# A decayed linear-attention layer feeding a cosine-gated MLP: another written order for the steps after the first two pairs of chunks

## The chip, the cores and the metric

The kernel runs on one core of a Trainium2 chip. The metric is the device time of one launch in microseconds (us), the median of several runs. The core has five engines that run side by side, each through its own queue in order: TensorE (PE, with its weight loads shown as PEld), VectorE (DVE), ScalarE (ACT), GpSimd (POOL) and SyncE (SP), which here only issues DMAs.

## The reference

For each of 4 sequences and 8 heads a 48x48 state is decayed and added to, position by position; the outputs of all heads are put side by side and go through an MLP whose gate is `h * cos(h)`.

```python
B, H, S, D = 4, 8, 768, 48          # q, k, v, alpha: (B, H, S, D)
for t in range(S):
    state = alpha[:, :, t, :, None] * state + einsum('bhd,bhe->bhde', k[:, :, t], v[:, :, t])
    y[:, :, t] = einsum('bhd,bhde->bhe', q[:, :, t], state)
x = y.transpose(0, 2, 1, 3).reshape(B * S, H * D)   # 3072 x 384
h = x @ w_in                                        # 3072 x 2048
out = (h * cos(h)) @ w_out                          # 3072 x 384
```

## The kernel before

**Tiles.** Positions are taken 256 at a time. Such a block is one *pair* J (two chunks c = 0, 1 of 128 positions); there are 12 pairs, three to a sequence, and J runs from 0. The step names below carry the pair and, behind a dot, the chunk or part: `m2.1.0 J6` is chunk 1, part 0 of the second products of pair 6.

**The steps of a pair**, each with the engine that it runs on by default:

- `load a/k/q/v` (SP): one DMA of 384 KB for each input. `mula` (POOL) multiplies neighbouring decays, `ln` (ACT) takes their logarithm, `cums` (PE, L156 and L168) sums the logarithms, `sub` (DVE, L183) subtracts.
- `eb` (ACT): two exponentials `icp` (L193), two exponentials `exps` (L201), and the `ln` (L142) of the next pair.
- `sk.e`, `sq.e` (POOL, or DVE where the plan has `:D`; L213, L217): k and q are scaled, even and odd positions e apart. `castv` (POOL) casts v, and `vst` (SP, four DMAs) stacks it in another layout; pair 2 does the latter with `vpe` on PE and `vev`. `decay` (POOL) prepares factors.
- `trans` (PE, L259) transposes the scaled k, then the scaled q; `evT.c` copies that out of PSUM. `scores.c` (PE, L273) and `mask.c` (DVE, L278) make the masked score matrix; `outer` (PE, L290), `add.c` (DVE) and `state.c` (POOL) carry the state.
- `yT` (PE, L339) makes the attention output transposed: first the products with the state, then those with the stacked v. `evy.c` copies it to `xT`.
- `m1.u` (PE, L360, 12 matmuls, u = 0 to 3): a quarter of the first product. `sin.u` (ACT, L366) is its cosine, `gate.u` (DVE, L371) multiplies both into `gsb`.
- `m2.c.part` (PE, L389, 4 matmuls each, four parts): the product with the second weights. `evo.c` (L401) copies it out and `out.c` (SP) stores it.

**What sets the order.** It is written out by hand: `PLAN` has for each step a row with one due number for each pair, the engine letter behind a colon where it is not the default. All steps are sorted by these numbers and recorded under `manual_schedule`, so each engine's queue holds its steps in the order of the numbers. The numbers are nothing but sort keys; an engine waits at the head of its queue until the inputs and the buffer are there, and whatever stands behind waits too.

**Buffers that tie the engines.** In PSUM three two-bank buffers with the tag `h` go round among `trans`, `scores`, `outer`, `yT` and `m1`: each needs what was taken three before it to have been read out. One bank (`o`) serves `m2`, so `m2.c.0` waits for the `evo` of the chunk before. One bank (`x`) serves `cums` and `vpe`. In SBUF, `k`, `q` and `v` have three buffers each (pair J+3 loads only when pair J has been scaled or cast), `a` has four. Between loads of the tables for exponentials and for the cosine, ACT needs an `ACT_TABLE_LOAD`.

```python
    order.append((int(t), len(order), kind, args))
    ...
        for _, _, kind, args in sorted(order, key=lambda x: x[:2]):
            steps[kind](*args)
```

Of the kernel before, what the change touches and what calls it, by code (L numbers as in the profile page):

```python
# [16 lines left out]
def kernel(  # L17
# [11 lines left out]
    B, H, S, D = q.shape  # L29
# [64 lines left out]
    w1 = [consts.tile([C, KT, DF // 2], BF, tag=f"w1{r}", name="w1") for r in range(2)]  # L94
# [316 lines left out]
    def idle(n):  # L411
# [18 lines left out]


    PLAN = {
# [66 lines left out]
    }  # L499
    IDLE = [(1201, 9), (6413, 2), (7383, 14), (11727, 1), (12377, 4), (15372, 5), (16939, 5), (20459, 1)]  # L500

# [44 lines left out]
```

## Time and profile before

| | us |
|---|---|
| median of 3 runs | 183.94 |
| lowest, highest | 183.26, 184.10 |
| the profiled execution, its time | 184.12 |
| the profiled execution, its span from first to last instruction | 182.3 |
| busy: PE, DVE, ACT, POOL | 175.4, 134.8, 129.9, 71.4 |

The profiled execution's time lies 1.8 us above its span, which is what lies around the kernel's own instructions, and 0.18 us above the median. A busy engine is one with an instruction in flight; for PE the ends of matmuls are modelled, so that short waits show best as the distance between starts. The granted TensorE clock is full over the whole span.

### The profile page before, as it was taken

The numbers are of one execution on the slowest core, as the hardware profiler recorded it, in microseconds if no ns is written. First come the engines' busy times: TensorE is split into PE (matmuls) and PEld (weight loads), VectorE is DVE, ScalarE is ACT, GpSimd is POOL, SyncE is SP. The second block draws the span as 40 slices with busy tenths as digits, with TensorE's granted clock in tenths as the row PEclk, the third lists the DMA queues.
The fourth block names the chain that finished last, engine by engine and source line by source line (L and its number), as shares of the span: only waits on it lengthen the run. The fifth ranks groups of instructions, "written<-read, shape, count | busy, mean of one in ns | idle before, by whom it ended". The sixth has DMA issues, their size and how long they took to land.

```text
span 182.3 us, 5756 instructions
## 1 busy us (share of the span) xinstructions
PE 175.4 (96%) x2467; PEld 132.6 (73%) x2470; DVE 134.8 (74%) x183; ACT 129.9 (71%) x169; POOL 71.4 (39%) x104
## 2 busy tenths in 40 slices
PE   7999899989999999998999999999999999999993
PEld 2455789746697877975799669686876796787872
DVE  7188878678879897599889886978688778363460
ACT  2837687998989999959578999838964174383331
POOL 5145830377777103734894298240720320100000
PEclk9999999999999999999999999999999999999999
DMA  5999999999989959996629905690052142010032
GB/s 148 261 261 220 199 215 221 273 260 265 248 184 283 249 132 295 289 277 202 147 63 229 273 18 166 155 233 0 4 110 83 45 109 81 4 43 4 0 129 86
DMA packets 57801, 29.47 MB, mean 162 GB/s; under 512 B 50992, under 2 KB 56496, under 8 KB 57776
## 3 DMA queue, kind: packets, MB, share of 16 engines
q1 hardware_dynamic: 56256, 25.86, 58.3%
q0 software_dynamic: 1376, 3.15, 9.3%
q8 instruction: 19, 0.31, 0.7%
q10 hardware_dynamic: 144, 0.10, 0.2%
q14 instruction: 6, 0.05, 0.1%
HBM read 25.17 MB, written 4.72 MB: 164 GB/s over the span
## 4 chain that ended last, share of the span: by engine, by line
PE 77%; ACT 11%; DVE 6%; DMA 2%; issue 2%; ACTq 0%
PE h_ps L360 29%; PE o_ps L389 28%; PE y_ps L339 5%; DVE gsb L371 5%; PE idle_ps L415 4%; ACT c_sb L366 3%; PE A_ps L273 3%; PE T_ps L259 3%; DMA a<-in_alpha_dram 2%; PE U_ps L290 2%; ACT L366 2%; PE o_last L383 1%; ACT L137 1%; ACT lna L142 1%; PE cums_h L156 1%
## 5 line engine op out<-in xcount | busy, mean ns | idle before, releaser
L371 DVE TENSOR_TENSOR gsb<-h_ps,c_sb 128x1024 bf16<-128x1024 f32 x48 | 58.2, 1222 | 20.8 <-ACT c_sb L366 19.4
L366 ACT ACTIVATE c_sb<-h_ps,halfpi 128x1024 bf16<-128x1024 f32 x48 | 53.3, 1115 | 26.7 <-PE h_ps L360 26.4
L389 PE MATMUL o_ps<-w,gsb 128*128 128x384 bf16 x368 | 67.1, 327 | 0.6 <-DVE o_sb L401 0.6
L360 PE MATMUL h_ps<-xT,w 128*128 128x256 bf16 x576 | 67.0, 273 | 0.3 <-issue 0.2
L360 PEld LDWEIGHTS <-w 128*128 128x128 bf16 x576 | 62.4, 114 | 2.5 <-DMA w<-in_moe_w_in_dram 0.3
L389 PEld LDWEIGHTS <-gsb 128*128 128x128 bf16 x368 | 33.9, 98 | 21.4 <-issue 1.1
L312 POOL TENSOR_TENSOR un<-us,c 128x384 bf16<-128x384 f32 x20 | 16.8, 838 | 46.2 <-DVE us L304 36.9
L278 DVE TENSOR_TENSOR A_sb<-A_ps,msk 128x1024 bf16<-128x1024 f32 x24 | 28.9, 1216 | 3.4 <-PE A_ps L273 3.4
L217 POOL TENSOR_TENSOR qh<-q,cp 128x384 bf16<-128x384 f32 x13 | 13.8, 1063 | 13.3 <-ACT cp L201 12.2
L213 POOL TENSOR_TENSOR kh<-k,icp 128x384 bf16<-128x384 f32 x15 | 14.9, 1007 | 2.4 <-ACT icp L193 1.0
L220 POOL CAST vp<-v 128x768 bf16<-128x768 f32 x12 | 9.9, 827 | 12.0 <-DMA v<-in_v_dram 12.0
L150 POOL TENSOR_TENSOR a<-a 128x384 f32<-128x384 f32 x9 | 9.0, 1003 | 10.1 <-DMA a<-in_alpha_dram 10.1
L142 ACT ACTIVATE lna<-a 128x768 bf16<-128x768 f32 x12 | 10.1, 844 | 3.5 <-DMA a<-in_alpha_dram 3.3
L415 PE MATMUL idle_ps<-zeros 128*128 128x512 bf16 x38 | 11.1, 439 | 1.4 <-DVE halfpi L77 1.2
L401 ACT COPY o_sb<-o_ps 128x384 f32<-128x384 f32 x13 | 6.2, 478 | 8.5 <-PE o_ps L389 8.5
L137 ACT ACT_TABLE_LOAD x9 | 11.5, 1283 | 0.9 <-PEq L530 0.7
L366 ACT ACT_TABLE_LOAD x9 | 11.5, 1283 | 0.2
L304 DVE TENSOR_TENSOR us<-U_ps,un 128x384 f32<-128x384 f32 x16 | 8.8, 551 | 3.8 <-POOL un L312 2.1
L265 ACT COPY qkT<-T_ps 128x1024 bf16<-128x1024 bf16 x10 | 9.8, 1016 | 1.9 <-PE T_ps L259 1.8
L217 DVE TENSOR_TENSOR qh<-q,cp 128x384 bf16<-128x384 f32 x11 | 6.8, 629 | 5.4 <-DMA q<-in_q_dram 5.3
L265 DVE COPY qkT<-T_ps 128x1024 bf16<-128x1024 bf16 x14 | 9.4, 680 | 1.2 <-PE T_ps L259 1.2
L273 PE MATMUL A_ps<-qkT 48*128 48x128 bf16 x192 | 9.0, 217 | 0.7 <-DVE gsb L371 0.5
(70 smaller groups left out, 156.6 us busy)
## 6 DMA issues: line engine op xcount, KB each, us to landing
a<-in_alpha_dram SPq DMA_DIRECT2D x12, 384.0 KB, 5.9
q<-in_q_dram SPq DMA_DIRECT2D x12, 384.0 KB, 6.1
k<-in_k_dram SPq DMA_DIRECT2D x12, 384.0 KB, 6.0
v<-in_v_dram SPq DMA_DIRECT2D x12, 384.0 KB, 6.3
out_dram<-o_sb SPq DMA_DIRECT2D x23, 192.0 KB, 3.5
vs<-vp SPq DMA_DIRECT2D x36, 64.0 KB, 2.8
w<-in_moe_w_in_dram POOLq DMA_DIRECT2D x2, 768.0 KB, 9.6
w<-in_moe_w_out_dram POOLq DMA_DIRECT2D x4, 384.0 KB, 8.7
```

The costliest lines, as they stand in the source:

```text
L137: nc.scalar.preload_act_table_set("natural_log_exp_and_others")
L213: eng.tensor_tensor(out=kh_t[J % NQ][:, e, :, 0:D], in0=kqv["k", J][:, :, e], in1=icp_, op=ALU.mult)
L217: eng.tensor_tensor(out=qh_t[J % NQ][:, e, :, 0:D], in0=kqv["q", J][:, :, e], in1=cp, op=ALU.mult)
L265: copy(out=qkT_sb[J][:, c], in_=T_ps[J][:, c].rearrange("r n e s -> r n (e s)"))
L273: nc.tensor.matmul(A_ps[J, c][:, a, p, :], qkT[r, c, NP + p, :], qkT[r, c, p, :], start=True, stop=True)
L278: nc.vector.tensor_tensor(out=A_sb[J][:, c].rearrange("s a p t -> s (a p) t"), in0=A_ps.pop((J, c)).rearrange("s a p t -> s (a p) t"), in1 ...
L312: nc.gpsimd.tensor_tensor(out=u, in0=U_sum.pop(n), in1=c2_sb[J][:, :, c].unsqueeze(3).to_broadcast([C, NP, 2, D]), op=ALU.mult)
L360: nc.tensor.matmul(h_ps[J, u][:, f, :], cols, xT[J][:, kk, :], start=(kk == 0), stop=(kk == KT - 1))
L366: nc.scalar.activation(out=c_sb[J, u], in_=h_ps[J, u], func=AF.Sin, bias=halfpi, scale=1.0)
L371: nc.vector.tensor_tensor(out=gsb[J][:, u * FW : (u + 1) * FW], in0=h_ps.pop((J, u)), in1=c_sb.pop((J, u)), op=ALU.mult)
L389: nc.tensor.matmul(o_ps[J, c][:, 0:DM], gsb[J][:, ft, c * C : (c + 1) * C], w2[:, ft], start=(ft == 0), stop=(ft == NF - 1))
L415: nc.tensor.matmul(idle_ps[0], zeros[:, 0:C], zeros, start=True, stop=True)
```

## The change

Only numbers and engine letters in `PLAN` differ: no step is added or taken away, no instruction has another shape. (The number of `w1` for pair 3 stands for nothing: `load_w1` returns for u above 1.) What it does:

- **Queue of PE, pairs 0 to 3.** `m1.2`, `m1.0`, `m1.1` of pair 1 come before the first `m2` of pair 0. `trans J2` goes ahead of `m2.0.0 J1`, `m2.0.1 J1` and `m2.0.2 J1`; `scores.1 J2`, `vpe`, `outer J2`, `trans J3` follow later. `cums J5` goes behind `m1.0 J2`.
- **Queue of PE, later.** `scores.1 J4` goes ahead of `m2.0.3 J2`; `cums J8` and `cums J11` go one `m2` block back; `outer J10` goes ahead of `scores.1 J11`; `m2.0.0 J10` goes ahead of `yT J11`. All else keeps its order.
- **DVE and ACT** exchange some copies: `evy.1` of pairs 1, 2, 8, `evy.0` of pairs 4, 10, `evT.0` of pairs 2, 10, `evo.0` of pairs 2, 8 and `evo.1 J9` go to DVE, `evo.1` of pairs 4, 8, `evo.0` of pairs 7, 9 and `evy.1 J9` to ACT. `gate.3 J1` now stands ahead of `evo.1 J0` on DVE.
- **POOL and DVE** exchange some scalings: `sk.0 J2`, `sq.0 J6`, `sk.1 J5`, `sq.0 J5`, `sq.1 J5`, `sq.0 J10`, `sk.1 J10`, `sq.1 J11` go to POOL, `sk.1 J3`, `sq.0 J3`, `sq.0 J9`, `sq.0 J11`, `sk.1 J11` to DVE (`sq.1 J3` to POOL).
- **SP**: loads, stacking copies and stores come in another order from the eleventh DMA on.

```diff
-        "load a": "750 2205 4425 24496 25066 37693 43693 45193 55293 56793 62293 70470",
-        "load k": "3345 7425 31693 34693 40693 52193 64033 73545 85258 93648 94218 114101",
-        "load q": "2775 8925 25636 36193 42193 52763 54533 63463 72180 78488 96723 113531",
-        "load v": "5925 10425 33193 39193 46693 64693 71040 71610 94788 95358 117164 132675",
+        "load a": "750 1320 4425 24496 31693 37693 42193 47393 55293 56793 60346 72793",
+        "load k": "2925 7425 25636 36193 45893 52893 65893 67033 84648 94083 97988 113396",
+        "load q": "1890 8925 25066 34693 40693 44393 54633 60916 71293 78478 93513 99488",
+        "load v": "5925 10425 33193 39193 54063 66463 70043 74293 85218 94653 95823 119529",
...
-        "cums": "5885 11199 13924 36668 44122 49975 61282 73275 86251 91443 105424 117024",
+        "cums": "5885 11199 13924 36015 44673 52476 61147 73140 86769 91308 105289 117542",
...
-        "sk 0": "9160:D 14846:D 39112:D 41953:D 48949 58577 77428:D 89268 92888 110613 111733 130015",
-        "sk 1": "9909:D 13739:D 38528 41528 47999 59591:D 73470 88318 91938 107448 124627:D 130965",
-        "sq 0": "7660:D 15296:D 37028:D 43028 52978 60646:D 77878:D 84607 93838 103437 116334:D 127345",
+        "sk 0": "9160:D 14846:D 37028 43028:D 55578 58442 77681:D 89133 92923 111493 112443 125569",
+        "sk 1": "9909:D 13739:D 37978 43478:D 52728 62842 74222 88183 91973 109423 121602 129221:D",
+        "sq 0": "7660:D 15296:D 35528:D 41528:D 54628 60162 77398 84472 93873 103302:D 114343 127138:D",
...
-        "castv": "12160 17628 40028 46545 56778 71528 75880 90218 100558 104387 129245 144989",
+        "castv": "12160 17628 40028 46500 59392 72502 76628 90083 96553 100423 123332 143936",
...
-        "trans": "10624 16461 40648 44533 57020 68793 81884 90868 108663 115899 126133 137709",
+        "trans": "10624 16461 39163 44098 56885 68658 81749 90733 108528 115764 125998 137574",
...
-        "evy 0": "19246 24739 49715 59116:D 72412 90700:D 90225:D 109076:D 125077:D 140194:D 150737 162583",
-        "evy 1": "18876 25109 49345 58036:D 72782 89595:D 90795 110156:D 124397 139114:D 150367 162953",
+        "evy 0": "19246 24739 49217 58506:D 72777:D 90565:D 90090:D 108941:D 124967:D 139939:D 151513:D 162978",
+        "evy 1": "18876 26020:D 48647:D 58981:D 72277 89460:D 90660 110021:D 124492:D 139204 150232 163348",
...
-        "gate 3": "27509 39826 56896 64334 79468 101000 112696 113876 137657 146554 162724 174200",
-        "m2 0 0": "28796 39247 55547 69368 82679 99651 110556 124292 136308 150139 162355 172851",
+        "gate 3": "27509 38291 56761 64114 79752 100865 112561 113741 137522 146419 162589 174065",
+        "m2 0 0": "31432 40041 55412 69233 82544 99516 110421 124157 136173 150004 161240 172716",
...
-        "evo 0": "34574:D 44322 62603 73475 85575 103280:D 116004 128413:D 140515 153925:D 165167:D 176969",
-        "evo 1": "38637:D 54119 68348:D 81659 92173:D 108601:D 123512 133462 144087:D 157621 171423 178295:D",
+        "evo 0": "34244:D 43548 61201:D 73728 85440 103752:D 115869 128079 140414:D 153556 165032:D 176834",
+        "evo 1": "39431:D 53684 68213:D 81524 91030 108466:D 123377 133327 143952 157486:D 168962 178160:D",
```

In the stretch that the change orders most freely, PE's queue reads as follows (before, then after):

```
m2.1.3 J0 | m2.0.0 m2.0.1 J1 | trans outer vpe.1 J2 | m2.0.2 J1 | vpe.0 scores.1 J2 | m2.0.3 J1 | cums J4 trans J3 scores.0 J2 | m2.1.0 m2.1.1 J1 | scores.0 J3 | m2.1.2 J1 | yT J2 scores.1 outer J3 | m2.1.3 J1 | cums J5 | m1 J2 ...
m2.1.3 J0 | trans J2 | m2.0.0 m2.0.1 m2.0.2 J1 | scores.1 vpe.1 J2 | m2.0.3 J1 | vpe.0 outer J2 trans J3 cums J4 | m2.1.0 J1 | scores.0 J2 scores.0 J3 | m2.1.1 m2.1.2 J1 | yT J2 scores.1 outer J3 | m2.1.3 J1 | m1.1 m1.0 J2 | cums J5 | m1 J2 ...
```

86 rows, old and new, of the table PLAN are left out of this document.

## The prediction

> **What bounds the kernel now.** I read the page's busy line and clock first, then the waits of PE, then the timeline of PE around each wait, and only then the other engines and the landings of the loads.
>
> ```profile
> PE 175.4 (96%) x2467; PEld 132.6 (73%) x2470; DVE 134.8 (74%) x183; ACT 129.9 (71%) x169; POOL 71.4 (39%) x104
> ...
> PEclk9999999999999999999999999999999999999999
> ```
>
> PE is the bound and runs at the full clock, so an order can gain only what PE spends waiting. The waits of PE behind the start (the head of the kernel, up to 21 us, keeps its order) are few:
>
> ```profile
> PE o_ps L389 <- DVE o_sb L401: 0.6, 1, 0.6
> PE A_ps L273 <- DVE gsb L371: 0.5, 1, 0.5
> ...
> PE U_ps L290 <- ACT xT L350: 0.3, 1, 0.3
> PE A_ps L273 <- DVE qkT L265: 0.2, 1, 0.2
> ```
>
> The two long ones in the timeline of PE (start, us, idle before it in brackets):
>
> ```profile
> 37.27 1.46 PE L389 MATMUL o_ps<-w,gsb 128*128 128x384 bf16 x8
> 39.38 1.46 PE L389 MATMUL o_ps<-w,gsb 128*128 128x384 bf16 x8 [0.65 <-DVE o_sb L401]
> ...
> 82.19 0.41 PE L259 MATMUL T_ps<-ident_bf,qh 64*128 64x64 bf16 x16
> 83.09 0.40 PE L273 MATMUL A_ps<-qkT 48*128 48x128 bf16 x8 [0.49 <-DVE gsb L371]
> ```
>
> By starts: eight products of `m2` take 1.40 us (39.38 to 40.78, where `trans J2` begins), so `m2.0.0 J1` could have begun at 37.27 + 1.40 = 38.67; it began at 39.38. The wait is 0.71. It is for the one `o` bank: `evo.1 J0` ran from 38.77 to 39.33. Scores follow a transpose's second half by 0.23 elsewhere (116.81 to 117.04), so `scores.1 J5` could have begun at 82.42; it began at 83.09, 0.67 late. Beyond these there are about 0.25 us at 117.4 and 0.16 at 25.1. All the waiting that an order could save behind the head is about 1.8 us, 1% of the time, while a new wait has no such cap.
>
> **Part 1, the front (38.7 to 50 us): a loss of 0.39.** The 48 first products and 32 second ones up to 38.67 change places, but I find each one's buffer in time: `m1.2 J1` at 27.9 needs `evy.1 J1`, now behind `gate.0 J0` (end 26.60) plus 0.59; `m1.0 J1` at 29.2 needs `gate.3 J0` (29.13); `m1.1 J1` at 30.5 needs `gate.2 J0` (30.44); `m2.0.2 J0` at 33.15 needs weights that landed at 33.03. Each margin is 0.05 to 0.7, and what slips here is caught by the wait that follows. Then `trans J2` comes ahead of `m2.0.0 J1`. Its k and q no longer wait behind two decay loads: q J2 and k J2 land in the second and third place, 35.65 and 37.10 (the slots in which alpha 4 and q J2 landed). POOL then does `sk.0 J2` and `sk.1 J2` from 37.13 at 1.00 us each, so PE may begin `trans J2` at 39.15 and spends 0.56 on it (68.88 to 69.44 in the trace). The `o` bank comes later than before, because `gate.3 J1` now stands ahead of `evo.1 J0` on DVE. ACT sets its time:
>
> ```profile
> 36.13 1.28 ACT L366 ACT_TABLE_LOAD   x1
> 37.42 1.11 ACT L366 ACTIVATE c_sb<-h_ps,halfpi 128x1024 bf16<-128x1024 f32 x1
> ```
>
> The cosine ends at 38.53, the gate takes 1.22 and ends at 39.8, `evo.1 J0` takes 0.56 with 0.08 of overlap and ends at 40.28, `m2.0.0 J1` begins at 40.33. PE's wait is 40.33 − 38.67 − 0.56 = 1.10 instead of 0.71: +0.39. Queued behind `evo.1 J0` are `evT.0 J2` and `evT.1 J2` (0.69 each, done at 41.7), which `scores.1 J2` wants at 42.4; `sk.0 J3` and `sk.1 J3` on DVE, with k J3 landing at 42.93, are done at 44.0 and `trans J3` wants them at 44.4; `yT J2` wants `mask.0 J2` at 47.9 and gets it at 47.4. The later pieces are the same work with as many changes of shape, so I see neither a second loss nor a gain up to `m1 J2`. Bounds: 0 (if the gate were to slip in earlier) to +0.7 (if k J3 is half a load slot late).
>
> **Part 2, the DVE queue at 77 us: a gain of 0.67.** What releases `scores.1 J5` is `gate.2 J4`, last of a row on DVE:
>
> ```profile
> 77.67 0.88 DVE L213 TENSOR_TENSOR kh<-k,icp 128x384 bf16<-128x384 f32 x1
> 78.47 1.18 DVE L217 TENSOR_TENSOR qh<-q,cp 128x384 bf16<-128x384 f32 x1
> 79.56 3.47 DVE L371 TENSOR_TENSOR gsb<-h_ps,c_sb 128x1024 bf16<-128x1024 f32 x3
> ...
> 78.39 0.84 POOL L220 CAST vp<-v 128x768 bf16<-128x768 f32 x1 [0.26 <-DMA v<-in_v_dram]
> ```
>
> The 1.18 us are `sq.0 J6`, which takes 0.56 when POOL is idle; it goes to POOL. Without it the gates of u = 0 and 3 follow at 78.5 and 79.7; the one of u = 2 waits for its cosine (79.75 + 1.11 = 80.86) and ends at 82.1, 0.3 before PE wants it at 82.42. So the wait goes entirely. Next late is nothing on DVE: `mask.1 J5` ends 0.6 ahead of `scores.0 J6`. The Trainium skill says in SBUF — State Buffer, "Who interferes with whom", that a DVE instruction with two SBUF inputs and a GpSimd instruction that reads SBUF lock each other out for a whole instruction. The trace agrees: `sq.0 J6` began 0.08 us behind a POOL cast of 0.84 and took 1.18, about the cast's rest and itself without its start-up. By the rule `sk.0 J6`, which stays, would fall to 0.56 too, which makes the gain safer and no larger.
>
> **Part 3, exchanged copies and queues moved past: a loss of 0.1, another 0.1 for the loads.** `evy.0 J4` on DVE waits for `evy.1 J4` on ACT, as both write one tile (at 91.3 us the trace shows the like: ACT waits 0.3 us for a DVE copy of `xT`). So 0.58 on ACT and 0.59 on DVE follow each other from 72.54 and `m1.1 J4` gets its input at 73.75, where PE came at 73.65: +0.1. The other exchanged copies have room: `evo.0 J8` 0.2 us, `evo.0 J7` 0.8, `evy.0 J10` over 2. The moved `cums` cost nothing (0.27 us between two `m2` blocks at 106.13 as in the row of others at 118.00), nor does `m2.0.0 J10` ahead of `yT J11`, whose copies are wanted 1.5 us later.
>
> On POOL, `sq.0 J6` now stands behind `castv J6`, which waits for v J6, and on SP the load of q J9 waits for `sq.0 J6`, and behind it stand one store and the eight stacking DMAs `vst J6` and `vst J5`. Before, v J6 landed at 78.33, the eight began at 81.84, and the last landed at 89.29; `yT J5` used it at 89.76. Afterwards v J6 has as many loads ahead (24) but two more stores, 0.57 us each (59.39 to 59.96). Against that, q J7 and alpha 10 go ahead of `vst J4`, so the hole of about 1.5 us that SP left in the transfers near 66 us (alpha 10 issued at 64.48, landed at 69.39) gets smaller. I take 78.8, between 78.3 and 79.4. Then `castv J6` and `sq.0 J6` end at 80.6, q J9 and the store are issued by 81.9, and the last stacked v lands at about 89.3, while PE, 0.3 us ahead of before, wants it at 89.5. Cost 0.1, bounds 0 and 0.4. Where k J4 comes three slots later (47.83 to about 52.6), POOL's four scalings end at 56.65 and `trans J4` wants them at 57.3.
>
> **The sum:** +0.39 − 0.67 + 0.1 + 0.1 = −0.08 on the profiled 184.12, so 184.04, and 183.9 at the median, which lies 0.18 lower. Two real changes cancel. About 0.5% (0.9 us) is what a measurement of this kernel can tell from no change.
>
> **Rivals.** First, slower: the chain v J6, `castv J6`, `sq.0 J6`, q J9, `vst J6`, `vst J5`, `yT J5`. It decides once v J6 lands after 79.1; from there every us goes to PE. One load slot (1.45 us) behind my 78.8 gives 80.25, so about 1.1 more; one and a half with `trans J6` itself late gives 185.2 to 185.6. For it: landings in the trace slip by 1 to 1.6 us now and then (q J6 came 2.6 us behind the store ahead of it). Against it: the shorter hole. 185.2, chance 0.20.
>
> Second, a wait that changes place: `sq.0 J9` is now on DVE ahead of `evo.0 J5`. It may begin at 104.3 (`exps` 103.76 + 0.52), end at 104.85, `evo.0 J5` at 105.35, and `m2.1.0 J5` comes at 105.47. It decides if a POOL cast of v J9 runs just then: 0.65 more, 184.5. v J9 is now the third load behind `vst J7`, a slot that landed at 103.12, and the cast ends at 104.0. By the lock rule named above this would be the full 0.65. Chance 0.08.
>
> Third, faster: the front costs nothing, since PE begins `trans J2` in its wait and the pieces behind it join better, and the transfers do no harm: 183.9 − 0.39 − 0.2 = 183.3, less if the wait at 117.4 goes as well (183.0). Against it: the ACT row is fixed by the landing of alpha 3, which stays. Chance 0.08.
>
> **How the numbers follow.** My forecast has 0.64, with 183.3 to 184.5 of its own from the bounds of its terms. Faster by over 0.5% means below 183.0: most of the third rival, 0.06. Slower by over 0.5% means above 184.9: the first rival and 0.04 of the forecast's own tail, 0.24. The rest, 0.70, lies within. The range 183.1 to 185.3 leaves out about a tenth on either side.
>
> **What would show it.** `m2.0.0 J1` at 40.3 behind an `evo` that follows `gate.3 J1`, with two waits of PE that make 1.1 us; no wait of `scores.1 J5` at 82; `m1.1 J4` waiting under 0.15; v J6 landed before 79.1. A wait of PE over 0.3 us anywhere from 42 to 82 us, or at `yT J5`, would make me wrong.

## The result, and the profile after

The changed kernel takes **184.17 us** (median of 20 runs, 183.62 to 184.80), the kernel before, measured beside it, **183.63 us** (20 runs, 183.16 to 184.34). The ratio is **1.0026, 95% interval 1.0016 to 1.0037**: slower by about half a microsecond, where the forecast was no change with a shade of gain. The shift is smaller than the 0.9 us that the prediction took for the least that can be told; twenty runs of each tell it. A second comparison, a5 below, gave 1.0028 (1.0010 to 1.0046). The median of 183.94 that the prediction started from, and its profiled execution (184.12), both stood above the median of 20.

The profiled execution of the changed kernel took 184.19, with a span of 182.4 against 182.3. Its busy line on the page:

```profile
PE 175.8 (96%) x2470; PEld 132.5 (73%) x2470; DVE 135.5 (74%) x184; ACT 127.4 (70%) x164; POOL 75.4 (41%) x108
```

PE is still the bound. The waits of PE (us in total, times, longest):

```profile
PE T_ps L259 <- POOL kh L213: 0.6, 2, 0.3
PE o_ps L389 <- DVE o_sb L401: 0.5, 1, 0.5
PE U_ps L290 <- ACT xT L350: 0.3, 1, 0.3
PE h_ps L360 <- issue: 0.3, 1, 0.3
```

The half microsecond of `scores.1 J5` behind a gate is gone, as forecast. One line is new: `trans` waits for scaled k from POOL. The first product `m1` waits for "issue", which is no wait for data; such a line of 0.2 us stood before too, but for a place in the head of the kernel (21.3 us), and now it is at 95.0. The timeline of PE (start, us, idle before it) shows four places:

```profile
38.94 0.38 PE L259 MATMUL T_ps<-ident_bf,kh 64*128 64x64 bf16 x14 [0.26 <-POOL kh L213]
39.16 0.40 PE L259 MATMUL T_ps<-ident_bf,qh 64*128 64x64 bf16 x16
40.01 1.30 PE L389 MATMUL o_ps<-w,gsb 128*128 128x384 bf16 x7 [0.46 <-DVE o_sb L401]
...
57.27 0.41 PE L259 MATMUL T_ps<-ident_bf,kh 64*128 64x64 bf16 x16 [0.32 <-POOL kh L213]
...
82.47 0.40 PE L259 MATMUL T_ps<-ident_bf,qh 64*128 64x64 bf16 x16
82.70 0.39 PE L273 MATMUL A_ps<-qkT 48*128 48x128 bf16 x8
...
92.06 2.68 PE L360 MATMUL h_ps<-xT,w 128*128 128x256 bf16 x23
95.00 1.17 PE L360 MATMUL h_ps<-xT,w 128*128 128x256 bf16 x9 [0.26 <-issue]
```

First the front: `m2.0.0 J1` at 40.01 (forecast 40.33). Then `trans J4` late at 57.27. Then `scores.1 J5` 0.23 behind the transposes, with no wait. Last, a hole inside one `m1` block: the weight loads of 23 matmuls, which elsewhere follow each other by 0.11 us, end at 94.47, and the next begins at 94.99.

POOL shows what `trans J4` waited for:

```profile
53.32 1.00 POOL L213 TENSOR_TENSOR kh<-k,icp 128x384 bf16<-128x384 f32 x1 [1.56 <-DMA k<-in_k_dram]
54.28 1.97 POOL L217 TENSOR_TENSOR qh<-q,cp 128x384 bf16<-128x384 f32 x2
56.20 1.01 POOL L213 TENSOR_TENSOR kh<-k,icp 128x384 bf16<-128x384 f32 x1
```

POOL stood 1.56 us for k J4, which landed at 53.18; its four scalings end at 57.21 instead of the forecast 56.65.

By starts of PE's steps in these two executions: `trans J4` cost 0.39 (0.23 of it is left at `m1.1 J3`), the hole at 94.5 us cost 0.45, and `scores.1 J5` gained 0.68. It would be easy to stop here with a tidy sum. The experiments show that each of these three numbers belongs to an execution rather than to the order.

### The profile page after: what moved, and what is told of

Its sections match the earlier page's. It is cut to its first block, busy times and chain, and to the rows that moved or that the text cites. A ratio compares the mean times of both kernels' runs of the same rounds, so it can differ in the third digit from the quotient of the medians.

```text
span 182.4 us, 5757 instructions
## 1 busy us (share of the span) xinstructions
PE 175.8 (96%) x2470; PEld 132.5 (73%) x2470; DVE 135.5 (74%) x184; ACT 127.4 (70%) x164; POOL 75.4 (41%) x108
## 4 chain that ended last, share of the span: by engine, by line
PE 72%; DMA 10%; ACT 9%; DVE 4%; POOL 2%; issue 1%; SPq 1%; ACTq 0%; POOLq 0%; DVEq 0%
PE h_ps L360 29%; PE o_ps L389 25%; DMA k<-in_k_dram 7%; PE idle_ps L415 4%; PE y_ps L339 4%; DVE gsb L371 3%; DMA a<-in_alpha_dram 3%; ACT c_sb L366 2%; PE T_ps L259 2%; PE A_ps L273 2%; PE U_ps L290 2%; PE o_last L383 1%; ACT L366 1%; ACT L137 1%; ACT lna L142 1%
## 5 line engine op out<-in xcount | busy, mean ns | idle before, releaser
L217 POOL TENSOR_TENSOR qh<-q,cp 128x384 bf16<-128x384 f32 x16 | 16.6, 1045 | 7.4 <-ACT cp L201 6.9
L213 POOL TENSOR_TENSOR kh<-k,icp 128x384 bf16<-128x384 f32 x16 | 15.9, 1009 | 4.7 <-ACT icp L193 3.0
L401 ACT COPY o_sb<-o_ps 128x384 f32<-128x384 f32 x14 | 6.7, 480 | 15.8 <-PE o_ps L389 15.8
L150 POOL TENSOR_TENSOR a<-a 128x384 f32<-128x384 f32 x9 | 9.0, 1004 | 12.5 <-DMA a<-in_alpha_dram 12.5
L415 PE MATMUL idle_ps<-zeros 128*128 128x512 bf16 x41 | 11.9, 431 | 1.2 <-DVE halfpi L77 1.2
L265 DVE COPY qkT<-T_ps 128x1024 bf16<-128x1024 bf16 x16 | 10.7, 683 | 1.5 <-PE T_ps L259 0.9
L350 DVE CAST xT<-y_ps 128x384 bf16<-128x384 f32 x14 | 7.9, 586 | 1.9 <-ACT xT L350 1.3
L265 ACT COPY qkT<-T_ps 128x1024 bf16<-128x1024 bf16 x8 | 7.8, 1015 | 1.9 <-PE T_ps L259 1.8
```

The costliest lines, as they stand in the source:

```text
L213: eng.tensor_tensor(out=kh_t[J % NQ][:, e, :, 0:D], in0=kqv["k", J][:, :, e], in1=icp_, op=ALU.mult)
L217: eng.tensor_tensor(out=qh_t[J % NQ][:, e, :, 0:D], in0=kqv["q", J][:, :, e], in1=cp, op=ALU.mult)
L265: copy(out=qkT_sb[J][:, c], in_=T_ps[J][:, c].rearrange("r n e s -> r n (e s)"))
L415: nc.tensor.matmul(idle_ps[0], zeros[:, 0:C], zeros, start=True, stop=True)
```

## The experiments

Times are given beside the kernel before on the same chip, as its median differed from chip to chip (183.54 to 183.89).

### Loads of k J4 and v J8

Three edits of the changed kernel: k J4 ahead of alpha J6; v J8 (which now stands right behind k J8) behind `vst J7`, with q J10 in exchange behind v J9; both.

```diff
-  load k J4  45893
+  load k J4  42100        (e1, e3)
-  load v J8  85218     load q J10 93513
+  load v J8  93400     load q J10 94700      (e2, e3)
```

> The changed kernel with one edit: the load of k J4 goes ahead of alpha J6, so that it lands near 49.2 us instead of 53.18. Theory (places add up, and the stall of PE at 94.5 us waits for something that comes at a fixed time): the wait of PE ahead of trans J4 (0.54 us in the changed kernel, 56.73 to 57.27) goes, PE is about 0.35 us ahead at 82 us, but PE then waits that much longer at 94.5 us, so the time stays at 184.1 us, not below 184.0. Rival A (each wait stands by itself): 183.8 us. Rival B (the front's order is the whole loss and the late k J4 costs nothing at the end): 184.2 us with no longer stall at 94.5 us.

> The changed kernel with the load of v J8 moved from its place right behind k J8 (issued at 88.35 us) to behind vst J7, and q J10 behind v J9 in exchange. Theory (PE runs out of instructions at 94.47 us, because the 16 KB packet with its next instructions, at 92.36 us, stood behind the load of v J8 on its DMA engine): the packet comes near 91.1 us as in the kernel before, PE has no gap inside m1 of pair 5, and the time falls by about 0.45, to 183.7 us. Rival (the gap of 0.5 us at 94.5 is chance, or belongs to something else than the load): the gap is still there in the profile or the time stays at 184.15 us.

> The changed kernel with both edits: k J4 loaded ahead of alpha J6, and v J8 behind vst J7. Theory: both waits of PE (0.54 us at 56.9, 0.52 us at 94.5) go, and the time falls by 0.7 to 0.85 us, to 183.3 to 183.45 us, below the kernel before at 183.63. Rival (the front, 38 to 50 us, is where the change loses): no more than 0.2 us below the changed kernel, 184.0 us.

| kernel | median | before beside it | ratio, 95% interval |
|---|---|---|---|
| e1, k J4 early | 183.88 | 183.54 | 1.0019 (1.0007 to 1.0031) |
| e2, v J8 late | 183.95 | 183.54 | 1.0021 (1.0007 to 1.0035) |
| e3, both | 183.76 | 183.54 | 1.0004 (0.9991 to 1.0017) |

With k J4 landing at 48.59, e1 has no wait at `trans J4`, but also no hole at 94.5 us, though v J8 stands where it stood; my theory for it, that PE would then stand longer at 94.5, fell. In e2 the hole is gone too, but so is the wait at `trans J4`, although k J4 keeps its place: it landed at 52.37. So neither of the two waits seems to come in every execution; the unchanged kernel, run again below, confirms it. In e3's profile something else came: v J6 landed at 79.28, the last of `vst J5` at 89.70, and `yT J5` waited for it, 0.66 us by starts up to `m1.1 J5`. The theories had expected 184.1, 183.7 and 183.3 to 183.45 us for the three; none came, and only e1's rival of 183.8 was near.

### One part alone: sq.0 J6 on POOL in the kernel before

The load of q J9, which waits for `sq.0 J6`, is moved along with it.

```diff
-  sq.0 J6  77878:D    load q J9  78488
+  sq.0 J6  77398      load q J9  93600
```

> The kernel before with one part of the change alone: sq.0 J6 goes from DVE to POOL behind castv J6; so that the stacking copies don't stand behind it, the load of q J9, which waits for it, goes behind vst J7. Theory: the wait of scores.1 J5 (0.67 us at 82.4) goes and nothing takes its place, so about 0.65 us less: 183.0 us. Rival (what is gained at 82 is given back at the next place where PE meets a late input, yT J5 or the instructions at 94 us): 183.4 to 183.6 us.

In the trace the stretch from `m1.1 J4` to `scores.1 J5` is 8.76 us instead of 9.44, and nothing later is late. The median is 183.49 beside 183.54, ratio 0.9994 (0.9981 to 1.0007): a wait of 0.67 was taken out and the median did not fall by more than 0.35, as the rival had it. Then most executions of the kernel before cannot have had it.

### The same orders again

Nothing but the number that stands for nothing was changed, for more executions of both kernels with a trace; and one variant of the kernel before exchanges the loads of v J6 and v J7.

```diff
-  w1 J3  45594             (b1, b3, b4: 45595 to 45597)
-  w1 J3  25095             (a2, a3, a4: 25096 to 25098)
-  load v J6  71040         (b2)
+  load v J6  71700
```

> The kernel before, unchanged in every instruction (only the number that stands for nothing differs): another execution, to see how much of the wait of scores.1 J5 (0.67 us at 82.4 in the first) belongs to that execution. Theory (chance of landing: sq.0 J6 on DVE took 1.18 us because v J6 landed at 78.33 and its cast on POOL fell upon it): where v J6 lands before 77.6 or after 79.1 us, sq.0 J6 takes 0.56 and the wait is at most 0.1 us; where it lands near 78.3, both are as before. Rival (the wait belongs to the order): 0.6 us or more again, wherever v J6 lands.

> The kernel before with the loads of v J6 and v J7 exchanged, so that v J6 lands one load later, near 79.0 to 79.8 us, when sq.0 J6 on DVE should be over. Theory (landing decides): sq.0 J6 takes 0.56 us, scores.1 J5 waits at most 0.1 us, and as the median execution of the kernel before hardly has that wait, the median stays within 0.2 us of it, 183.4 to 183.7 us. Rival (the order decides): the wait stays at 0.6 us; a cost may come at yT J5, where v J6 later means stacked v later (185 us).

> The changed kernel, unchanged in every instruction (only the number that stands for nothing differs): another execution. Theory (the wait of trans J4 for k J4 and the gap of 0.5 us at 94.5 us belong to the first execution, the front and m1.1 J4 to the order): from m2.1.3 J0 to yT J2 9.8 to 10.1 us, m1.1 J3 to m1.1 J4 9.50, no gap inside m1.1 J5, and yT J2 to trans J4 9.3 us unless k J4 lands after 52.6. Rival (the two belong to the order): both are there again, with 0.3 us or more each.

> The kernel before, a third execution. Theory (landing decides): the stretch from m1.1 J4 to scores.1 J5 is 8.76 us, or more only where the cast of v J6 falls upon sq.0 J6; where it is 8.76 us, yT J5 is reached 0.7 us earlier and waits 0.2 to 0.5 us for vst J5 if v J6 lands after 78 us. Rival (the order decides): 9.44 us again.

> The kernel before, a fourth execution. Theory and rival as for the third: 8.76 us from m1.1 J4 to scores.1 J5 unless a cast falls upon sq.0 J6, against 9.44 us in every execution.

> The changed kernel, a third execution. Theory: m2.1.3 J0 to yT J2 9.6 to 10.1 us, m1.1 J3 to m1.1 J4 9.50, m1.1 J4 to scores.1 J5 8.75, no gap at 94.5 us; yT J2 to trans J4 9.3 us, or longer by what k J4 lands after 52.6 us. Rival (the gap at 94.5 us belongs to the order): 1.76 us from m1.1 J5 to m1.0 J5 in place of 1.31.

> The changed kernel, a fourth execution. Theory and rival as for the third: trans J4 late only by what k J4 lands after 52.6 us and no gap at 94.5 us, against both in every execution.

The timeline of DVE in the second execution of the kernel before:

```profile
77.51 0.55 DVE L213 TENSOR_TENSOR kh<-k,icp 128x384 bf16<-128x384 f32 x1
77.98 0.55 DVE L217 TENSOR_TENSOR qh<-q,cp 128x384 bf16<-128x384 f32 x1
78.44 3.52 DVE L371 TENSOR_TENSOR gsb<-h_ps,c_sb 128x1024 bf16<-128x1024 f32 x3
```

and of POOL and PE in the same one:

```profile
76.52 1.00 POOL L150 TENSOR_TENSOR a<-a 128x384 f32<-128x384 f32 x1
78.35 0.86 POOL L220 CAST vp<-v 128x768 bf16<-128x768 f32 x1 [0.83 <-DMA v<-in_v_dram]
```

```profile
82.02 0.40 PE L259 MATMUL T_ps<-ident_bf,qh 64*128 64x64 bf16 x16
82.26 0.39 PE L273 MATMUL A_ps<-qkT 48*128 48x128 bf16 x8
...
88.84 0.28 PE L339 MATMUL y_ps<-A_sb,vs 128*32 128x128 bf16 x5
89.30 0.55 PE L339 MATMUL y_ps<-A_sb,vs 128*32 128x128 bf16 x25 [0.18 <-DMA vs<-vp]
```

v J6 landed at nearly the same time as in the first (78.30 against 78.33), but DVE was half a microsecond earlier: `sq.0 J6` had begun 0.37 us ahead of the cast and took 0.55 instead of 1.18. Most of that half comes from a second meeting that only the first execution had: POOL's `mula` (L150) ran there from 77.13 to 78.13, beside `sk.0 J6`, which took 0.88; here it was over when `sk.0 J6` began, and that took 0.55. So the row of gates ends in time, `scores.1 J5` waits for nothing, and PE comes to `yT J5` 0.84 earlier than in the first execution, and stands there until the stacked v of 89.16 is in. In the third execution the cast fell upon the other scaling, `sk.0 J6` (DVE, then POOL):

```profile
77.42 1.19 DVE L213 TENSOR_TENSOR kh<-k,icp 128x384 bf16<-128x384 f32 x1
78.54 0.55 DVE L217 TENSOR_TENSOR qh<-q,cp 128x384 bf16<-128x384 f32 x1
```

```profile
77.38 0.82 POOL L220 CAST vp<-v 128x768 bf16<-128x768 f32 x1 [0.26 <-DMA v<-in_v_dram]
```

and there `scores.1 J5` was 0.36 us late. In the fourth (cast at 76.40) neither was lengthened, nor, but for 0.16 us, in the variant b2 (cast at 79.74), where `yT J5` paid 0.78 (up to `m1.1 J5`) for the later v J6 instead; b2's time is that of the kernel before within the noise (184.00 beside 183.89, ratio 1.0000, 0.9981 to 1.0020). I had written that the landing of v J6 alone decides, with 78.3 as the harmful value; b1 landed there and had no wait. What decides is which of the two engines begins first. The Trainium skill says so in SBUF — State Buffer, "Who interferes with whom": issue order decides who blocks. All these traces agree, with 0.55 us against 1.18 and 1.19. A trace from below (f3) shows the reverse: there `sk.0 J6` began 0.08 us ahead of the cast and kept its 0.55, and the cast took 1.16 instead of 0.82.

The stretches of PE in all executions of the two plain orders (a5, below, is the fifth of the changed one):

| from, to | before (4) | changed (5) | difference of means |
|---|---|---|---|
| start to yT J2 | 47.62, 47.48, 47.38, 47.44 | 47.58, 47.45, 47.39, 47.45, 47.70 | +0.04 |
| yT J2 to m1.1 J3 (k J4) | 16.68, 16.67, 16.68, 16.68 | 16.86, 17.21, 16.97, 16.63, 16.63 | +0.18 |
| m1.1 J3 to m1.1 J4 (evy.0 J4) | 9.35 in each | 9.51, 9.51, 9.51, 9.50, 9.50 | +0.16 |
| m1.1 J4 to m1.1 J5 (82 us, yT J5) | 20.13, 19.85, 19.81, 19.72 | 19.42 in four, 20.09 | −0.32 |
| m1.1 J5 to m1.0 J5 | 1.31 in each | 1.76, 1.31, 1.31, 1.31, 1.61 | +0.15 |
| m1.0 J5 to the last m2 | 83.31 to 83.32 | 83.33 to 83.34 | +0.02 |

They sum to +0.23. The times of these nine executions have means of 183.73 and 183.96. Of the measured half microsecond the table explains that part; it is a mean of few executions that spread over 1.2 us, and the rest is not pinned to a place. The traced executions are not typical either: three of the five of the changed kernel took less than 184.0 us, but only 3 of its 20 timed runs.

The variants help with the sample. Three of them (e2, e6, f2) have the changed order untouched up to `yT J2`, and it began there at 48.18, 48.03 and 47.93. With them the front's mean is 47.71, a loss of 0.23 over eight traces and not 0.04. The wait at `trans J4` is 0.17 over the nine traces that load k J4 in the changed place, and the hole 0.08 over the nine that load v J8 there. With the other rows as they are the sum is +0.34, at the lower end of what the ratio's interval allows, 0.29 to 0.68 us.

One sum does not close. e4's stretch from `m1.1 J4` to `m1.1 J5` takes 19.43, so by the four traces of the kernel before e4 should be 0.45 faster, and its median was 0.05 faster, 0.35 at most. A handful of traces gives the places of the waits, not their weights. Of the expectations, the front of a2 and a3 (`m2.1.3 J0` to `yT J2` 9.65 and 9.39 us) came out below the 9.8 and 9.6 that they had, and b3's 9.12 comes from `sk.0 J6`, where only `sq.0 J6` had been named.

### The load that waits for sq.0 J6

```diff
-  load q J9  78478
+  load q J9  93400     (e6; e5: 93600, with both edits of e3)
```

> The changed kernel with that last edit alone: q J9 behind vst J7. Theory (floor at yT J5 in a share of the executions): 0.1 to 0.3 us less than the changed kernel, 183.9 to 184.05 us. Rival (k J4 and the packet of instructions cost everything, and the floor is not felt as long as PE comes late): 184.15 us.

> The changed kernel with three edits in SP's queue: k J4 ahead of alpha J6, v J8 behind vst J7 (q J10 behind v J9), and q J9, which waits for sq.0 J6 on POOL, behind vst J7 instead of ahead of vst J6. Theory (the stacked v of pair 5 sets a floor for yT J5 in a share of the executions, as in the profile of the kernel with two edits, where the last of vst J5 landed at 89.70 and yT J5 waited 0.45 us): the last of vst J5 lands 0.5 us or more earlier for the same landing of v J6, no wait at yT J5, and the median falls from 183.76 to 183.4 us. Rival (the front holds the rest of the loss): 183.7 us.

e6: 184.03 beside 183.89, ratio 1.0001 (0.9986 to 1.0016). e5: 184.00, ratio 1.0007 (0.9989 to 1.0026), so it missed its 183.4. e6's ratio is below the changed kernel's 1.0026, with intervals that just touch, but e5, which holds the same edit, is not as low. e5's trace shows the edit at work: v J6 landed at 79.47, later than anywhere in the changed order, and yet the last of `vst J5` landed at 88.21 and `yT J5` did not wait. The times spread too much to put a price on it.

### The front and the copies of xT

```diff
-  gate.3 J1  38291
+  gate.3 J1  39600      (f1)
-  evy.0 J4   72777:D
+  evy.0 J4   72200      (f2)
```

> The changed kernel with gate.3 J1 put back behind evo.1 J0 in the queue of DVE. From m2.1.3 J0 to yT J2 the traces of the kernel before and its variants take 9.70 to 9.78 us, those of the changed kernel and its variants 9.84 to 10.06 (one 9.38, whose start was 0.6 us late). Theory (the o bank comes late because evo.1 J0 stands behind a gate that waits for its cosine): the wait of m2.0.0 J1 (0.46 to 0.58 us) goes, the stretch takes 9.5 to 9.6 us, and the time falls by 0.3 to 0.45 us, to 183.7 to 183.85 us where the changed kernel is at 184.17. Rival (the copies evT J2, which then stand behind the gate, come later, and scores.1 J2 waits instead): the stretch stays at 9.9 to 10.0 us and the time at 184.1 us.

> The changed kernel with evy.0 J4 back on ACT, ahead of evy.1 J4. From m1.1 J3 to m1.1 J4 every trace of the kernel before's order takes 9.35 us, every one of the changed order 9.50 to 9.51. Theory (the two copies of one tile on two engines wait for each other): 9.35 us again, and 0.15 us less in all, 184.0 us, which is at the edge of what the times can tell. Rival (the 0.15 us come from another step): 9.50 us again.

f1's timeline of PE:

```profile
39.00 0.38 PE L259 MATMUL T_ps<-ident_bf,kh 64*128 64x64 bf16 x14 [0.28 <-POOL kh L213]
39.22 0.40 PE L259 MATMUL T_ps<-ident_bf,qh 64*128 64x64 bf16 x16
39.55 1.64 PE L389 MATMUL o_ps<-w,gsb 128*128 128x384 bf16 x9
```

With `gate.3 J1` behind `evo.1 J0` the wait for the `o` bank is gone, here and in f3 and f4 below, so what makes `m2.0.0 J1` late is shown. The stretch from `m2.1.3 J0` to `yT J2` is 9.52 us, the shortest of the changed order but for two executions with a late head; f3 and f4, with the same edit, took 10.11 and 9.65, so what the edit is worth at `yT J2` is not shown. f2's stretch from `m1.1 J3` to `m1.1 J4` is 9.35 us, so the cost of `evy.0 J4` on DVE is shown. The times tell neither, and both are above what was expected: 184.14 (ratio 1.0019, 0.9997 to 1.0041) and 184.50 (1.0020, 0.9998 to 1.0042). In f2's profile k J4 landed at 54.11 and `trans J4` stood 0.88 us, the most of all.

### All edits together

```diff
+  gate.3 J1 39600, evy.0 J4 72200, load k J4 42100,
+  load v J8 93400, load q J9 93600, load q J10 94700
```

> The changed kernel with all the edits so far: gate.3 J1 behind evo.1 J0, evy.0 J4 on ACT, k J4 ahead of alpha J6, v J8 and q J9 behind vst J7 (q J10 behind v J9). Theory (front +0.26, m1.1 J4 +0.15, and waits for loads in a share of the executions): all of it gone, 183.25 to 183.4 us where the kernel before is at 183.6. Rival (what is gained in the front is caught up at the next late input): the same as the kernel before, 183.6 us.

> The changed kernel once more, timed in five rounds beside the kernel before. Theory (the loss is a sum over executions of waits that come and go with the landings: front +0.2, k J4 +0.2, m1.1 J4 +0.15, the gap at 94.5 +0.06, and -0.4 for the waits at 82.4 and yT J5 of the kernel before): slower by 0.2 us, ratio 1.000 to 1.003. Rival (a constant loss of 0.5 us that the traces don't show): 1.003 or more.

> The version with all the edits once more, on the same chip. Theory: m1.1 J4 costs nothing, k J4 and the stacked v of pair 5 are in time in every execution, and what stays is the landing of k J3 ahead of trans J3; 0.2 to 0.4 us faster than the kernel before, 0.4 to 0.7 us faster than the changed kernel. Rival (the edits only moved the waits): the same as the changed kernel within 0.2 us.

| kernel | median | before beside it | ratio, 95% interval |
|---|---|---|---|
| f3, all edits | 183.55 | 183.76 | 0.9985 (0.9967 to 1.0002) |
| a5, the changed kernel | 184.46 | 183.83 | 1.0028 (1.0010 to 1.0046) |
| f4, all edits | 183.56 | 183.83 | 0.9983 (0.9972 to 0.9994) |

f4 is 0.9 us below a5 on one chip and a little faster than the kernel before. So the six edits together take the loss away; which takes how much, the single edits could not resolve. a5's ratio of 1.0028 is nearer to its rival's 1.003, a loss that the traces don't show, than to the 0.2 us of its theory, and its interval takes in both, so that rival is not excluded. a5's profile (time 184.60) shows two of them at once. PE, then PEld:

```profile
89.21 0.29 PE L339 MATMUL y_ps<-A_sb,vs 128*32 128x128 bf16 x5
89.87 0.55 PE L339 MATMUL y_ps<-A_sb,vs 128*32 128x128 bf16 x25 [0.38 <-DMA vs<-vp]
```

```profile
93.92 1.09 PEld L360 LDWEIGHTS <-w 128*128 128x128 bf16 x10
95.39 0.69 PEld L360 LDWEIGHTS <-w 128*128 128x128 bf16 x7 [0.38 <-issue]
```

v J6 had landed at 79.13 and the last of `vst J5` at 89.74, which cost 0.67 up to `m1.1 J5`; and the hole inside `m1.1 J5` is there again. In f4 the waits at `trans J4`, `m1.1 J4`, `yT J5` and 94.5 us are all absent; about 0.4 us by starts went for `add.1 J3` ahead of `m1.2 J2` and, in f3, 0.4 us for k J3, which landed at 43.20.

## Why the prediction was wrong, step by step

- **Part 2, a gain of 0.67: the step that failed.** The mechanism was read rightly: `sq.0 J6` lengthened by a POOL cast, the row of gates late, the wait gone when it moves; 8.75 us in all five executions of the changed order. What was wrong is to take the 0.67 of one execution as what the median has. The four executions of the kernel before waited 0.68, 0, 0.36 and 0 there, 0.26 in the mean. "Next late is nothing" failed too: with the wait gone `yT J5` meets its stacked v, in two of those executions for 0.42 and 0.29 us (up to `m1.1 J5`). The stretch up to `m1.1 J5` gained 0.32 in the mean, half of the term; and e4, the move with its load, gained 0.05 at the median (0.35 at most). That `sk.0 J6` "would fall to 0.56 too" held in the five, with 0.55, but it is a matter of timing as well: in e4 the cast fell upon it and it took 1.03, without harm to `scores.1 J5`.
- **k J4, "POOL's four scalings end at 56.65 and trans J4 wants them at 57.3".** Mis-sized on both sides. k J4 landed at 52.03 to 53.42 in the five executions, with 52.6 forecast, and PE wants the scalings at about 56.8, so the slack was 0.2 and not 0.6. Three of five executions paid, 0.18 in the mean.
- **Part 1, a loss of 0.39.** The order of events was right: `m2.0.0 J1` behind an `evo` that follows `gate.3 J1`, at 39.81 to 40.12 in the five executions against the forecast 40.33. The cost up to `yT J2` was only 0.04 in these five, since much was given back by the pieces behind; in the six variants with that front `yT J2` began at 47.62 to 48.18 against 47.48 before, up to 0.7 more, which is the bound that was given, and over the eight traces with the same order up to there the cost is 0.23. So the term was too large, by how much is open. With the gate put back `m2.0.0 J1` began at 39.55, 39.41 and 39.69 (f1, f3, f4) against a mean of 39.94, so its place is worth 0.25 to 0.5 us at that step.
- **m1.1 J4, 0.1:** 0.16 in every execution, and 9.35 again in f2. Right, a little small.
- **The loads, 0.1, and the first rival.** v J6 was forecast at 78.8 and landed at 78.36 to 79.13. The first rival's chain is what struck a5, at 79.13, for 0.67, and e3, at 79.28, for 0.66. Its point of decision, 79.1, was too late: by its rule, every us behind 79.1 goes to PE, these two would have paid 0.03 and 0.18. In a5 the stacked v of 89.74 was wanted at about 89.3, where the prediction had 89.5. f2, at 79.14, paid nothing: its stacked v landed at 89.31. That one of five plain executions paid, as many as the chance of 0.20, is luck.
- **Not foreseen: the hole at 94.5 us,** 0.45 and 0.30 in two of five executions. No term of the sum and no rival has it.
- **The second rival did not come:** everything behind `m1.0 J5` took the same within 0.03 us in all nine, `evo.0 J5` included. Nor did the third: the front cost less than its term, but k J4 and the hole took that back.

So the mean over executions is −0.32 + 0.18 + 0.16 + 0.15 + 0.06 = +0.23, where the forecast had −0.08, and the sign turns with the one term that was read off a single execution. What stays open is the other 0.3 of the measured 0.54, or 0.2 if the front, `trans J4` and the hole are counted over the variants too.

## What to carry to other kernels

A wait in a profile is a sample. Before a gain is booked for removing it, ask whether its cause is the order or a coincidence of a landing with an instruction; if two events have to meet within half a microsecond, book a share of it. And a later load is not paid for by the mean slack: where a queue like POOL's stands behind it, the spread of the landings (here 1.4 us for k J4) is paid on one side only.

## What was not expected of the hardware

In two executions PE seems to have run out of instructions. The page of the changed kernel lists what brings them as a DMA queue of its own:

```profile
q8 instruction: 19, 0.31, 0.7%
```

These are 19 packets of 16 KB for the 4,972 recorded PE instructions, one for each 260 or so, so I take them to be PE's. The packet that belongs to the hole began at 92.36 us in the changed kernel and took 1.18, and PE went on at 94.99; in a5 it began at 92.63, took 1.19, and PE went on at 95.39: 1.45 and 1.57 us behind the packet's end. The instruction at which PE stood is the same: record 2,753, and 2,750 in a5, whose trace holds three records fewer, from the idle matmuls of the head. In the other 18 traces that packet began between 89.81 and 92.25 and there was no such hole. In a3 it was just in time: its packet ended at 92.97, and the same record began at 94.43, 1.46 us later and 0.05 us late. The packets are late where v J8 stands behind k J8: 90.56 to 92.63 in the nine traces of that order, 89.81 to 91.12 in the eleven others. That the load holds the packet up is thus likely but not shown: PE's own lateness also shifts the packet, and no run added the load alone. The Trainium skill says in Runtime: NRT & Kernel Launch, "Instruction fetch mechanics", that crossing such a block costs one bump of a DMA tail, mostly hidden. Here, if the packets are what they are taken for, it was hidden in 18 of 20 traces at this place, but for the 0.05 us of a3, and cost 0.45 and 0.30 us in two.
